# Moving a sign merge of the weight rounding from VectorE to GpSimd in every other piece

## The chip, the cores and the metric

The kernel runs on one core of a Trainium2 chip. The metric is the device time of one execution in microseconds (us): the median of three runs of the kernel before is 1490.21 us (1490.04 to 1492.53). The profile shown below is of one execution whose span is 1490.6 us.

The core's engines each work through a list of instructions in a fixed order: TensorE (PE) multiplies matrices, VectorE (DVE) does elementwise work and sorting steps, ScalarE (ACT) does activations and copies, GpSimd (POOL) does elementwise work more slowly, SyncE (SP) issues the transfers (DMA). [...]

## What is computed

```python
scores = scale * np.matmul(q, k.transpose(0, 1, 3, 2))      # 8 x 8 heads, 576 x 576 each
kth = np.partition(scores, -32, axis=-1)[..., -32:-31]
scores = np.where(scores >= kth, scores, -1e9)              # the 32 largest of each row stay
attn = softmax(scores)                                       # in words: exp, divided by the row's sum
x = (attn @ v), laid out as 4608 tokens x 512
h = x @ w_in                                                 # 512 x 2048
out = np.maximum(0.01 * h, h) @ w_out                        # 2048 x 512
```

The weights `w_in` and `w_out` arrive as float64. The kernel takes each as four 16-bit words and makes the float32 itself: that is the weight rounding, and the change is in it.

## The kernel before

**The opening.** The two weight matrices are cut into 16 pieces (`NPIECE`) of 128 x 1024 numbers, 1 MB each as float64. `load_weights` (L95 to L102) brings a piece into a tile `raw`, of which there are three buffers. `round_weights` (L104 to L149) is a Python generator that emits one piece's rounding in three steps:

- Step 0. GpSimd copies the highest of the four words of each number into a dense tile `top` (L119). ScalarE turns the second word into a part of the significand (L120, straight into the weight tile) and the two lowest words into another (L122).
- Step 1. VectorE takes the exponent out of `top` (L124), clamps it (L126); ScalarE shifts it to the place of a bfloat16's exponent (L128; for the last two pieces VectorE does it, L130). The result, `scale`, is a power of two written as a bfloat16. VectorE makes the leading bits of the significand (L131) and then leaves in `top` only the sign bit (L132). TensorE adds the three parts of the significand up in PSUM (L142 to L144).
- Step 2. VectorE puts the sign into `scale` with a bitwise or of two 16-bit tiles (L146), and multiplies the sum in PSUM by it (L149). The product is the float32 weight.

The loop at the end of the kernel runs the steps as a software pipeline: in round n it emits step 0 of piece n, step 1 of piece n-1, step 2 of piece n-2, and then the load of piece n+3. Each engine executes its own part of this in the order written. So VectorE's list repeats a block of six: L124, L126, L131, L132 of one piece, then L146 and L149 of the piece before it.

`top` and `scale` have two buffers each. A tile of piece n takes the place of piece n-2's, so GpSimd's copy L119 of piece n waits until L146 of piece n-2 has read its `top`. Rounds 6 to 9 also load queries and keys; round 13 and the end of the loop compute the scores of the first two attention units (`first_scores`), whose copies (L231) go through ScalarE's list.

**The main part.** After the rounding, 144 attention units follow, one a slot. VectorE finds the 32 largest of each row (L240, L245, L248), GpSimd masks (L258, L259), ScalarE takes exponents, normalizes and splits the result into 16-bit halves (tile `split`, two buffers, L283) for a transposing transfer; TensorE computes scores, weighs the values (L323), and runs the matrix products with the weights (L374, L386) in between. VectorE begins this part only when its list of the rounding is empty.

Of the kernel before, what the change touches and what calls it, by code (L numbers as in the profile page):

```python
# [10 lines left out]
U16 = mybir.dt.uint16  # L11
BF16 = mybir.dt.bfloat16
AF = mybir.ActivationFunctionType
ALU = mybir.AluOpType
# [5 lines left out]
def kernel(  # L20
# [13 lines left out]
    nc = tc.nc  # L34
    NPAIR, P, S = qT.shape
# [14 lines left out]
    WCH = 1024  # L50
# [10 lines left out]
    raws = ctx.enter_context(tc.tile_pool(name="raws", bufs=3))  # L61
    work = ctx.enter_context(tc.tile_pool(name="work", bufs=2))
# [20 lines left out]
    AS_WORDS = weights.dtype != F32  # L83

    def piece(n):

        if n < NPIECE // 2:
            j, c = divmod(n, HP)
            return w_in[c][:, j * WCH:(j + 1) * WCH]
        f = 2 * (n - NPIECE // 2)  # L90
        return w_out[f // 4][:, f % 4:f % 4 + 2, :].rearrange("p g n -> p (g n)")
# [3 lines left out]
    def load_weights(n):  # L95
        if n >= NPIECE:
            return
        if not AS_WORDS:
            nc.sync.dma_start(piece(n), weights[n])
            return  # L100
        raw_of[n] = raws.tile([P, WCH, 4], U16, name="raw")
        nc.sync.dma_start(raw_of[n].rearrange("p n w -> p (n w)"), weights[n])  # L102

    def round_weights(n):  # L104

        raw = raw_of.pop(n)  # L110
        dst = piece(n)
        mid = raw[:, :, 2]
        low = raw.rearrange("p n w -> p (n w)").bitcast(U32).rearrange("p (n w) -> p n w", w=2)[:, :, 0]
        top = raws.tile([P, WCH], U16, name="top", bufs=2)
        scale = raws.tile([P, WCH], U16, name="scale", bufs=2)
        parts = work.tile([P, 2 * NKC - 1, P], F32, name="wT", bufs=3)
        parts = parts.rearrange("p c n -> p (c n)").bitcast(U16)
        m_top, m_low = parts[:, 0:WCH], parts[:, WCH:2 * WCH].bitcast(BF16)
        nc.gpsimd.tensor_copy(top, raw[:, :, 3])  # L119
        nc.scalar.activation(dst, mid, AF.Copy, bias=-7.0 - 2.0 ** -16, scale=2.0 ** -20)  # L120

        nc.scalar.activation(m_low, low, AF.Copy, bias=128.0, scale=2.0 ** -29)  # L122
        yield
        nc.vector.tensor_scalar(scale, top, 4, 0x7FF, ALU.logical_shift_right, ALU.bitwise_and)  # L124

        nc.vector.tensor_scalar(scale, scale, 1151.0, 896.0, ALU.min, ALU.max)  # L126
        if n < NPIECE - 2:
            nc.scalar.activation(scale, scale, AF.Copy, bias=-896.0 * 128, scale=128.0)  # L128
        else:
            nc.vector.tensor_scalar(scale, scale, 896.0, 128.0, ALU.subtract, ALU.mult)  # L130
        nc.vector.tensor_scalar(m_top, top, 0xF, 0x3F80, ALU.bitwise_and, ALU.bitwise_or)  # L131
        nc.vector.tensor_scalar(top, top, 0x8000, None, ALU.bitwise_and)  # L132
        if n < NPIECE - 4 or n % 2 == 0:
            tag, bufs = ("wide", 2) if n < NPIECE - 4 else ("narrow", 1)
            pw = ps_sc.tile([P, 2, 512], F32, name=tag, bufs=bufs)
            sums = [(pw[:, h, :], h * 512) for h in range(2)]
            ends = [(pw.rearrange("p h n -> p (h n)"), 0)]
        else:
            ends = sums = [(ps_ml.tile([P, 512], F32, name="pw", tag="ml"), h * 512) for h in range(2)]
        for pw, c in sums:  # L140
            at = slice(c, c + 512)
            nc.tensor.matmul(pw, ident_top, m_top[:, at].bitcast(BF16), start=True, stop=False)  # L142
            nc.tensor.matmul(pw, ident, dst[:, at], start=False, stop=False)
            nc.tensor.matmul(pw, ident_low, m_low[:, at], start=False, stop=True)  # L144
        yield
        nc.vector.tensor_tensor(scale, scale, top, ALU.bitwise_or)  # L146
        for pw, c in ends:
            at = slice(c, c + pw.shape[-1])
            nc.vector.tensor_tensor(dst[:, at], pw, scale[:, at].bitcast(BF16), ALU.mult)  # L149
# [5 lines left out]
    def load_qk(pi):  # L155
        qt = loads.tile([P, S], F32, name="qt")
        kt = loads.tile([P, S], F32, name="kt")
        nc.sync.dma_start(qt, qT[pi])
        nc.sync.dma_start(kt, kT[pi])
        qk_of[pi] = qt, kt  # L160
# [58 lines left out]
    def first_scores(u):  # L219

        ps = [ps_sc.tile([P, 2, 512], F32, name="wide", bufs=2) for i in range(2)]
        for half in range(2):
            for i, pi, side, r0 in u.parts:
                qt, kt = qk_of[pi]
                d = slice(side * D, (side + 1) * D)
                nc.tensor.matmul(ps[i][:, half, 0:HS], qt[d, u.q0:u.q0 + P],
                                 kt[d, half * HS:(half + 1) * HS], start=True, stop=True)
        u.both = work.tile([P, 2, S], F32, name="s_sb", bufs=5)
        u.s = [u.both[:, i, :] for i in range(2)]
        for i in range(2):  # L230
            nc.scalar.copy(u.s[i].rearrange("p (h n) -> p h n", h=2), ps[i][:, :, 0:HS])  # L231
# [201 lines left out]
    def unit(n):  # L433
        return steps[n] if 0 <= n < len(steps) else None
# [26 lines left out]
    with tc.manual_schedule():  # L461
        last = {p: n for n, u in enumerate(steps) for p in u.pairs}

        def load_more(s):

            for of, load, n, lag in ((qk_of, load_qk, LOADED, -2), (v_of, load_v, LOADED_V, LAG + 1)):
                while len(of) < NPAIR and (len(of) < n or last[len(of) - n] + lag <= s):
                    load(len(of))


        for n in range(3):
            load_weights(n)
        rounding = {}
        for n in range(NPIECE + 2):
            for i in (n, n - 1, n - 2) if AS_WORDS else ():
                if 0 <= i < NPIECE:
                    if i == n:
                        rounding[i] = round_weights(i)
                    next(rounding[i], None)
            load_weights(n + 3)  # L480
            if 6 <= n < 6 + HP:
                load_qk(n - 6)
            elif n == NPIECE - 3:
                first_scores(steps[0])
            elif n == NPIECE:
                first_scores(steps[1])
            if n == NPIECE - 1:
                load_v(0)
                load_v(1)

        def values(s):
            due = [u for n, u in enumerate(steps) if values_at(n) == s]
            if due:
                po = ps_sc.tile([P, 2, 512], F32, name="wide", bufs=2)[:, 0, 0:2 * P]
                po = po.rearrange("p (u n) -> p u n", u=2)
            else:
                return
            for part in (weigh_values, keep_values):
                for n, u in enumerate(due):
                    part(u, po[:, n, :])  # L500
            attended(s)

        for s in range(len(steps) + LAG + 1):
            cur, old, older, new = unit(s), unit(s - 1), unit(s - 2), ()
            if s % 2 == 0:
                new = [u for u in steps[s + 2:s + 4] if u]
            picks = top_k(cur) if cur else iter(())
            budget = slot_budget(s)

            def slot():  # L510
                next(picks, None)

            slot()
            if old:
                mask(old, 0)
                mask(old, 1)
            if older:
                reciprocals(older)
                normalize(older, 0)
                normalize(older, 1)  # L520
            mlp_steps(budget)
            slot()
            if s - 2 in HURRIED:
                transpose_in_haste(older)
            mlp_steps(budget)
            if old:
                exponents(old, 0)
            if older:
                keep_transposed(older) if s - 2 in HURRIED else transpose(older)
            slot()  # L530
            mlp_steps(budget)
            mlp_steps(budget)
            slot()
            mlp_steps(budget)
            if old:
                exponents(old, 1)
                sums(old)
            if new and s < HURRY:
                scores(new)
            values(s)  # L540
            if new and s >= HURRY:
                scores(new)
            budget = slot_budget(s + 1)
            mlp_steps(budget)
            mlp_steps(budget)
            load_more(s)
        mlp_steps(1e9)
# [58 lines left out]
```

## Time and profile before

| Stretch of the span, us | PE busy | DVE busy | ACT busy | POOL busy | DMA share |
|---|---|---|---|---|---|
| 0 to 13.3 (first pieces) | 5.29 | 4.29 | 8.67 | 4.19 | 0.86 |
| 13.3 to 69.5 (rounding, steady) | 43.47 | 52.10 | 42.05 | 14.82 | 0.79 |
| 69.5 to 113 (first attention units) | 7.92 | 43.15 | 22.95 | 30.14 | 0.22 |
| 113 to 1440 | 1298.33 | 1229.35 | 1017.21 | 1048.48 | 0.54 |
| 1440 to 1490.6 | 46.83 | 0.00 | 4.75 | 0.00 | 0.03 |

Each cell but the last column is the time in us in which the engine had an instruction in flight during the stretch; the last column is the mean busy share of the core's 16 DMA engines. The stretches were chosen where the work changes: at 13.3 us VectorE writes its first finished weights, at 69.5 us it begins with the attention. An engine whose busy time fills a stretch is a candidate for what sets its length; whether it does is told by the chain of waits, not by this table.

### The profile page before, as it was taken

The numbers are of one execution on the slowest core, as the hardware profiler recorded it, in microseconds if no ns is written. First come the engines' busy times: TensorE is split into PE (matmuls) and PEld (weight loads), VectorE is DVE, ScalarE is ACT, GpSimd is POOL, SyncE is SP. The second block draws the span as 40 slices with busy tenths as digits, with TensorE's granted clock in tenths as the row PEclk, the third lists the DMA queues.
The fourth block names the chain that finished last, engine by engine and source line by source line (L and its number), as shares of the span: only waits on it lengthen the run. The fifth ranks groups of instructions, "written<-read, shape, count | busy, mean of one in ns | idle before, by whom it ended". The sixth has DMA issues, their size and how long they took to land.

```text
span 1490.6 us, 24127 instructions
## 1 busy us (share of the span) xinstructions
PE 1401.8 (94%) x8077; PEld 934.0 (63%) x8077; DVE 1328.9 (89%) x3414; ACT 1095.6 (74%) x1979; POOL 1097.6 (74%) x742
## 2 busy tenths in 40 slices
PE   6708977999999999999999999999999999999998
PEld 2305546666666766676766666767676767676674
DVE  7999998999999999999999999999999999999600
ACT  8647786777788877777777777777777777777720
POOL 2277787888788887788887888888878887788700
PEclk9968997999999999999999999999999999999999
DMA  8623354635566566655564566545765465645510
GB/s 325 249 64 84 99 166 122 169 110 145 156 162 160 142 163 170 171 134 165 168 177 126 137 168 171 164 142 155 177 163 142 130 168 147 169 128 142 143 47 14
DMA packets 386172, 221.12 MB, mean 148 GB/s; under 512 B 331520, under 2 KB 331520, under 8 KB 384000
## 3 DMA queue, kind: packets, MB, share of 16 engines
q1 hardware_dynamic: 386048, 219.59, 52.5%
q8 instruction: 63, 1.03, 0.3%
q14 instruction: 61, 0.50, 0.1%
HBM read 46.14 MB, written 91.42 MB: 92 GB/s over the span
## 4 chain that ended last, share of the span: by engine, by line
PE 84%; DVE 6%; ACT 4%; DMA 4%; issue 1%; SPq 0%; POOL 0%; DVEq 0%; ACTq 0%
PE pz L386 34%; PE ph L374 28%; PE wide L323 11%; PE wide L210 6%; PE narrow L210 3%; DMA wT<-apart 2%; ACT split L283 2%; DMA apart<-split 1%; DVE tops L245 1%; ACT s_sb L274 1%; DVE pairs L248 1%; ACT s_sb L262 1%; PE ph L348 1%; DVE w_out L149 1%; DVE w_in L149 1%
## 5 line engine op out<-in xcount | busy, mean ns | idle before, releaser
L258 POOL TENSOR_SCALAR pen<-s_sb,tops 128x576 f32<-128x576 f32 x288 | 638.3, 2216 | 223.7 <-DVE tops L245 136.0
L245 DVE MAX8 tops<-pairs 128x8 f32<-128x288 f32 (+1 forms) x1152 | 636.4, 592 | 0.0
L386 PE MATMUL pz<-w_out,gT 128*128 128x512 f32 x1152 | 508.3, 596 | 1.4 <-ACT gT L359 1.4
L374 PE MATMUL ph<-x,w_in 128*128 128x256 f32 x2176 | 481.1, 381 | 0.0
L248 DVE MATCH_REPLACE8 pairs<-tops,pairs 128x288 f32<-128x288 f32 (+1 forms) x864 | 460.5, 539 | 0.0
L374 PEld LDWEIGHTS ph<-x,w_in 128*128 128x128 f32 x2176 | 410.7, 190 | 77.1 <-issue 22.9
L259 POOL TENSOR_TENSOR s_sb<-s_sb,pen 128x576 f32<-128x576 f32 x288 | 406.8, 1413 | 24.0
L386 PEld LDWEIGHTS pz<-w_out,gT 128*128 128x128 f32 x1152 | 215.3, 190 | 266.2 <-issue 263.4
L283 ACT COPY split<-s_sb 128x1152 uint16<-128x1152 uint16 x278 | 304.8, 1145 | 0.0
L262 ACT ACTIVATE s_sb<-s_sb,nbias 128x576 f32<-128x576 f32 x288 | 221.1, 768 | 12.4 <-POOL s_sb L259 12.4
L274 ACT ACTIVATE s_sb<-s_sb,rz 128x576 f32<-128x576 f32 x288 | 207.1, 770 | 25.6 <-DVE rz L271 25.6
L240 DVE TENSOR_TENSOR pairs<-s_sb 128x576 f32<-128x576 f32 x288 | 213.7, 780 | 9.9
L323 PEld LDWEIGHTS wide<-wT,vt 128*64 128x64 f32 x3200 | 164.5, 141 | 66.0 <-issue 18.7
L323 PE MATMUL wide<-wT,vt 128*64 128x128 f32 (+1 forms) x3200 | 183.3, 271 | 23.2 <-ACT s_sb L217 15.1
L337 ACT COPY x<-wide 128x128 f32<-128x128 f32 (+1 forms) x160 | 32.3, 261 | 153.3 <-PE wide L323 153.3
L210 PE MATMUL wide<-kt,qt 64*128 64x352 f32 (+1 forms) x632 | 118.3, 488 | 27.5 <-ACT s_sb L217 22.0
L380 ACT ACTIVATE gT<-ph 128x512 f32<-128x512 f32 x136 | 80.7, 593 | 78.8 <-PE ph L374 78.8
L217 ACT COPY s_sb<-wide 128x704 f32<-128x704 f32 x142 | 107.0, 754 | 21.7 <-PE wide L210 21.7
L210 PEld LDWEIGHTS wide<-kt,qt 64*128 64x128 f32 (+1 forms) x632 | 48.6, 178 | 44.8 <-ACT s_sb L217 22.5
L210 PE MATMUL narrow<-kt,qt 64*128 64x224 f32 (+1 forms) x632 | 69.1, 358 | 7.7 <-DMA kt<-in_kT_dram 7.7
L271 DVE RECIPROCAL rz<-ze 128x2 f32<-128x2 f32 x144 | 22.5, 156 | 60.2 <-ACT ze L267 60.0
L217 ACT COPY s_sb<-narrow 128x448 f32<-128x448 f32 x142 | 68.7, 536 | 5.6 <-PE narrow L210 4.9
(58 smaller groups left out, 551.0 us busy)
## 6 DMA issues: line engine op xcount, KB each, us to landing
apart<-split SPq DMA_DIRECT2D x278, 288.0 KB, 2.1
raw<-in_weights_dram SPq DMA_DIRECT2D x16, 1024.0 KB, 6.0
vt<-in_vk_dram SPq DMA_DIRECT2D x32, 320.0 KB, 3.3
qt<-in_qT_dram SPq DMA_DIRECT2D x32, 288.0 KB, 3.7
kt<-in_kT_dram SPq DMA_DIRECT2D x32, 288.0 KB, 4.0
out_dram<-o_sb SPq DMA_DIRECT2D x36, 256.0 KB, 2.0
wT<-apart SPq DMA_TRANSPOSE x139, 4.6
```

The lines of the kernel that those rows point to most:

```text
L210: nc.tensor.matmul(to[r0:r0 + u.rows, i, :], qt[d, u.q0:u.q0 + u.rows], kt[d, k0:k1], start=True, stop=True)
L240: nc.vector.tensor_tensor(pairs[:, :, n, :], u.both[:, :, 0:HS], u.both[:, :, HS:S], op)
L245: nc.vector.max(out=u.tops[:, i, r, :], in_=rest[i])
L248: nc.vector.match_replace(out=rest[i], in_to_replace=u.tops[:, i, r, :], in_values=rest[i], imm_value=LOWEST)
L258: nc.gpsimd.tensor_scalar(pen, u.s[i], u.tops[:, i, ROUNDS - 1, 7:8], MASKED, ALU.is_lt, ALU.mult)
L259: nc.gpsimd.tensor_tensor(u.s[i], u.s[i], pen, ALU.add)
L262: nc.scalar.activation(u.s[i], u.s[i], AF.Exp, bias=u.nbias[:, i:i + 1], scale=SCALE, accum_out=u.z[:, i:i + 1])
L274: nc.scalar.activation(u.s[i], u.s[i], AF.Copy, bias=0.0, scale=u.rz[:, i:i + 1])
L283: nc.scalar.copy(split, pairs[:, :, h])
L323: nc.tensor.matmul(po[side * D:(side + 1) * D, o, :], vt[:, c, side, :], u.wT[:, c + side * NKC if c + 1 < NKC else c, r:r + n], start=(c ...
L374: nc.tensor.matmul(ph[:, i, 0:n], w_in[c][:, f * P:(f + 1) * P], x[c][:, 0:n], start=(c == 0), stop=(c == HP - 1),)
L386: nc.tensor.matmul(pz[0:m, 0:DMODEL], gT[:, f, r0:r0 + m], w_out[f // 4][:, f % 4, :], start=(f == 0), stop=(f == NFC - 1),)
```

## The change

The sign merge of step 2 moves to GpSimd for the odd pieces. There, VectorE's L132 leaves not the bare sign bit but the bfloat16 number +1 or -1 (sign bit, and the bits 0x3F80 of 1.0), and GpSimd multiplies `scale` by it as bfloat16 numbers, which puts the sign on the power of two. Even pieces keep the bitwise or on VectorE. The aim is to take an instruction off VectorE's block in every other piece.

So that GpSimd's list can run further ahead, the highest words get four buffers in all: two of the tile `top` as before, and, for pieces with n % 4 of 2 or 3, the two buffers of the attention's tile `split`, which is not in use yet. The copy L119 of piece n then waits for the reader of piece n-4's words. The generator gets a fourth step: the product of piece n-2 is emitted first in round n, ahead of the copy of piece n in GpSimd's list; VectorE's L146 and L149 stay at the round's end.

```diff
-        top = raws.tile([P, WCH], U16, name="top", bufs=2)
+        if n % 4 < 2:
+            top = raws.tile([P, WCH], U16, name="top", bufs=2)
+        else:
+            top = work.tile([P, 2 * S], U16, name="split", bufs=2)[:, 0:WCH]
...
-        nc.vector.tensor_scalar(top, top, 0x8000, None, ALU.bitwise_and)
+        if n % 2:
+            nc.vector.tensor_scalar(top, top, 0x8000, 0x3F80, ALU.bitwise_and, ALU.bitwise_or)
+        else:
+            nc.vector.tensor_scalar(top, top, 0x8000, None, ALU.bitwise_and)
...
         yield
-        nc.vector.tensor_tensor(scale, scale, top, ALU.bitwise_or)
+        if n % 2:
+            nc.gpsimd.tensor_tensor(scale.bitcast(BF16), scale.bitcast(BF16), top.bitcast(BF16), ALU.mult)
+        yield
+        if n % 2 == 0:
+            nc.vector.tensor_tensor(scale, scale, top, ALU.bitwise_or)
...
-            for i in (n, n - 1, n - 2) if AS_WORDS else ():
+            for i in (n - 2, n, n - 1, n - 2) if AS_WORDS else ():
```

## The prediction

> **What bounds the kernel now.** I read the table of stretches first (in the section on the profile), then the chain of waits of the first 130 us, then VectorE's and GpSimd's lists in order of time. The diff touches only the opening, and there the chain, followed back from 130 us, runs through VectorE from 13.3 to 69.5 us without a break. One block of it, from the chain (start, time on the chain, what):
>
> ```profile
> 22.09 0.44 DVE scale L124
> 22.55 0.43 DVE scale L126
> 22.98 0.35 DVE wT L131
> 23.35 0.43 DVE top L132
> 23.77 0.61 DVE scale L146
> ...
> 24.48 1.24 DVE w_in L149
> 25.81 0.44 DVE scale L124
> ```
>
> L124 to L132 belong to piece 4, L146 and L149 to piece 3. The block repeats after 25.81 - 22.09 = 3.72 us, as it does until 59 us, and VectorE waits for nothing in it. Start to start in VectorE's list (L132 at 23.35, L146 at 23.69), the four 16-bit instructions take 1.60 us ("the four" from here on), L146 0.79, L149 1.33. The rest has room: ScalarE's three take about 3.05 (L128 starts at 10.14, 13.11 and 16.15), TensorE's six 2.58.
>
> GpSimd is idle two thirds of the time, but look at when it runs (start, duration, then what ended its idle time):
>
> ```profile
> 5.60 1.10 POOL L119 COPY top<-raw 128x1024 uint16<-128x1024 uint16 x1 [4.31 <-DMA raw<-in_weights_dram]
> 8.09 1.30 POOL L119 COPY top<-raw 128x1024 uint16<-128x1024 uint16 x1 [1.39 <-DMA raw<-in_weights_dram]
> ...
> 20.72 1.14 POOL L119 COPY top<-raw 128x1024 uint16<-128x1024 uint16 x1 [2.58 <-DVE scale L146]
> 24.44 1.15 POOL L119 COPY top<-raw 128x1024 uint16<-128x1024 uint16 x1 [2.57 <-DVE scale L146]
> ```
>
> In the steady state each copy starts as L146 ends and lies wholly beside L149 (24.48 to 25.71). The wait for `top`, 2.6 us a time, keeps the copies out of the way of the four. The only copy that met one of them is the second: it started at 8.09 inside L132 (7.99 to 8.42) and took 1.30, not 1.10.
>
> After 69.5 us everything starts from VectorE's first L240, so I count each us gained or lost in the opening as one us of the end.
>
> [...]
>
> Does the trace show the exclusion? GpSimd waiting for VectorE: yes, the 1.30 us copy. VectorE waiting for GpSimd: the main part shows it for the two-input L240 (two of them in the row of 948.88, which take about 1.5 elsewhere):
>
> ```profile
> 948.88 1.80 DVE L240 TENSOR_TENSOR pairs<-s_sb 128x576 f32<-128x576 f32 x2
> ```
>
> ```profile
> 948.67 2.22 POOL L258 TENSOR_SCALAR pen<-s_sb,tops 128x576 f32<-128x576 f32 x1 [2.19 <-ACT split L283]
> ```
>
> L240 by itself takes 745 ns; the longest of all 288 takes 1136 and is the first of these two, with L258 begun 0.21 us before it. It was held 0.39 us, to 0.60 after L258's start, not for L258's whole 2.22. So the exclusion is real[...]. That one of the four[...] is held to GpSimd's end is not shown anywhere here.
>
> [...] L259, two f32 inputs of 576, takes 1.41[...].
>
> **The change, part by part.**
>
> - *L146 gone for odd pieces*: -0.79 us a block in every other block. A pair of blocks would take 2 x 3.72 - 0.79 = 6.65 instead of 7.44.
> - *L132 with a second operation*: L124 has two operations and 0.43 us, L132 one and 0.43. Nothing.
> - *The product on GpSimd*: not in the trace. Nearest row: L259, 1.41 x 1024/576 = 2.51. Low end 1.14, a copy of as many 16-bit elements with one input; high end 3.94, L258 by elements (2216 ns x 1024/576). I take 2.5: same instruction[...].
> - *Four buffers*: L119 loses its wait for L146. Copies, and with them the release of `raw`, come earlier, but nothing on the chain waits for either; what they do is move the copies out from beside L149.
> - *New waits*: the product waits for L128 and L132 of its piece; behind it in GpSimd's list stand the copies of the next two pieces, on which L124 of those pieces hangs. L149 of an odd piece waits for the product; behind it is VectorE's whole list.
>
> GpSimd's work per pair is 2.5 + 2 x 1.12 and three gaps of 0.1, 5.0 us, beside a pair of 6.65. If nothing contended it would fit. With exclusion I walk one pair, time 0 at L124 of an odd piece. The four end at 1.60. L146 of the even piece before runs 1.60 to 2.28[...]. L128 of the odd piece is done at 0.92 + 1.06 = 1.98, so the product starts as L146 ends, 2.32, beside L149 (starts 2.39), and ends at 4.83. VectorE wants its next four at 3.72: it **waits 1.11**. They run 4.83 to 6.43, then L149 of the odd piece to 7.76. The first queued copy [...] runs to about 7.6; the second follows at 7.7, just ahead of the next L124, and ends at 8.85: VectorE **waits 1.1** again. The pair takes 8.9 us: 7.44 - 0.79 + 1.11 + 1.1. Should L124 win that race instead, the second copy falls behind the next L146 and the product behind the copy, and the wait that the product causes grows by about the same 1.1: again 8.9.
>
> So +1.45 us a pair. Of the eight products, the first (piece 1) falls where VectorE waits for a cold TensorE anyway (1.42 us at 13.32), so I count seven: 7 x 1.45 = +10.2. At the very end L149 of piece 15 can start 0.43 + 2.5 + 0.1 = 3.03 after L132's start at 65.26; before it started at 68.31, 3.05 after. That end is a wash. Likeliest: 1490.2 + 10.2 = **1500.4**.
>
> **The rivals.**
>
> - *No hold on the four by GpSimd* (faster). For: the hold on L240 ended after 0.6 of 2.2 us, and no trace here shows one of the four held. Against: [...]the copy held by L132. Then six products save 0.79, -4.7; piece 13's comes late, because its L128 stands behind the first scores' copies in ScalarE's list (it ran at 60.23 before, 3.8 us after the end of its L126), and 2.6 us of product replace 0.79 of L146: +0.9, half of the difference, as all of ScalarE's list also moves ahead. Sum -3.8: 1486.4; from 1484.7 (seven savings) to 1489.
> - *Half a hold*: [...] The two waits shrink to 0.7 and 0.9: pair 8.25, +0.8 x 7 = +5.7: 1495.9.
> - *A worse order*: both copies fall between the four, not beside L149. Pair 6.65 + 1.11 + 2 x 1.12 = 10.0, +2.56 x 7 = +18: 1508. For it: the four have gaps of some hundredths between dependent ones, in which a queued copy could get in. Against: a copy that is ready as the four end falls beside L149 by itself.
>
> A product of 1.14 or 3.94 us would shift the likeliest case by about -1.1 x 7 = -8 (the first wait gone) or +1.4 x 7 = +10[...].
>
> **How the numbers follow.** Full hold 0.41, half a hold 0.22, worse order 0.10, no hold 0.27. "Faster" (under 1487.2) takes 0.16 of the no-hold case, "same" its other 0.11 and 0.05 of a half hold with a quick product; the rest, 0.68, is slower. The range 1486 to 1508 leaves out the better part of no hold, about 0.1, and the slower part of the worse order with a slow product, about 0.1.
>
> **What would show it.** The start of VectorE's first L240, 69.52 before, should be about 80, and the end should move with it. In the steady opening the block should alternate, with idle time before L124 or L126[...]: GpSimd's product or a copy in flight up to the moment at which it starts, or durations well above 0.43. If the four keep 0.43 us beside a running product and the pair takes 6.65, the no-hold case is right and I am wrong. If the product takes far from 2.5 us, the sum is off by that. A shift of L240 that the end doesn't show would refute the one-for-one count.

## The result, and the profile after

The changed kernel takes 1505.38 us (median; 1503.49 to 1505.64), against 1491.37 us for the kernel before on the same chip: 1.0089 times as long, interval 1.0072 to 1.0107. That is 13.3 us more (10.7 to 16.0). Its profiled span is 1503.4 us, 12.8 more than before.

In the lines of the changed kernel, the four are L127, L129, L134 and L136 or L138 (L136 in odd pieces, with the second operation); the even pieces' merge is L156, the multiplication out of PSUM L159, ScalarE's shift of the exponent L131, GpSimd's copy L122, its product L153, the first attention instruction L250.

The table of stretches, cut at 13.3 us as before and at VectorE's first attention instruction, tells where the time is (the stretch and its length, PE busy, PE loads, DVE, ACT, POOL, each with its number of instructions, then the TensorE clock, DMA share, GB/s). The first line is of the kernel before, the second of the changed one:

```profile
13.30:69.50 56.20, 43.47 (x136) 17.64 (x135) 52.10 (x91) 42.05 (x42) 14.82 (x13) 1.00 0.79 303
13.30:82.70 69.40, 49.35 (x133) 19.75 (x133) 60.21 (x84) 41.73 (x42) 33.63 (x21) 0.88 0.66 247
```

The stretch lasts 69.4 us instead of 56.2. So a loss of 13.2 us is made in the rounding, and the span's 12.8 says that it is carried to the end. VectorE has fewer instructions there (84 for 91), yet its busy time has *grown*, from 52.1 to 60.2 us. So 8.1 us of the loss show up as busy time and don't look like a wait; the other 5.1 are idle time, 4.13 of it in one wait at the end of the rounding. The clock column, 1.00 before and 0.88 now, is a second thing to come back to.

The chain of waits of the same block that the prediction opened with (start, time on the chain, what):

```profile
24.49 0.86 DVE scale L127
25.38 1.20 DVE scale L129
26.57 1.25 DVE wT L134
28.19 1.23 DVE w_in L159
29.51 0.44 DVE scale L127
```

Three of the four, 0.43 us each before, show 0.86, 1.20 and 1.25, and the block takes 29.51 - 24.49 = 5.02 us instead of 3.72. Why, is told by VectorE's and GpSimd's instructions in order of time (start, duration; in brackets idle time and what ended it):

```profile
22.37 0.69 DVE L156 TENSOR_TENSOR scale<-scale,split 128x1024 uint16<-128x1024 uint16 x1
...
22.89 2.17 POOL L153 TENSOR_TENSOR scale<-scale,split 128x1024 bf16<-128x1024 bf16 x1 [3.64 <-DMA raw<-in_weights_dram]
23.16 1.23 DVE L159 TENSOR_TENSOR w_in<-wide,scale 128x1024 f32<-128x1024 f32 x1
...
24.49 0.85 DVE L127 TENSOR_SCALAR scale<-top 128x1024 uint16<-128x1024 uint16 x1
...
25.00 1.28 POOL L122 COPY top<-raw 128x1024 uint16<-128x1024 uint16 x1
25.38 1.20 DVE L129 TENSOR_SCALAR scale<-scale 128x1024 uint16<-128x1024 uint16 x1
26.23 1.29 POOL L122 COPY split<-raw 128x1024 uint16<-128x1024 uint16 x1
...
26.49 1.32 DVE L134 TENSOR_SCALAR wT<-top 128x1024 uint16<-128x1024 uint16 x1
...
27.85 0.43 DVE L138 TENSOR_SCALAR top<-top 128x1024 uint16<-128x1024 uint16 x1
```

Follow GpSimd. Its product of piece 3 starts at 22.89, 0.08 us after its exponent L131 is done (21.75 + 1.06) and while piece 2's merge L156 is still in flight (the bracket names a transfer, which the product doesn't read; in the next pairs it names L131). It lies beside L159 without harm (1.23, as ever), and ends at 25.06. L127 begins inside it and ends at 25.34; it takes 0.42 longer than its 0.43. The copy of piece 5 follows and ends at 26.28; L129 takes 1.20. The copy of piece 6 ends at 27.52; L134 takes 1.32. Then GpSimd's list is empty and L138 has its 0.43. Each of the three gets through as one GpSimd instruction ends and, while it runs, holds the next one up: the copies take 1.28 and 1.29, against 1.10 to 1.16 in the kernel before, away from the four. The three rows name neither idle time nor a releaser: a held instruction has started, has no idle time before it, and is counted as busy.

### The profile page after: what moved, and what is told of

The parts are those of the page before. It is cut to its first block, busy times and chain, and to the rows that moved or that the text cites. A ratio compares the mean times of both kernels' runs of the same rounds, so it can differ in the third digit from the quotient of the medians.

```text
span 1503.4 us, 24132 instructions
## 1 busy us (share of the span) xinstructions
PE 1408.3 (94%) x8077; PEld 934.9 (62%) x8077; DVE 1338.2 (89%) x3406; ACT 1095.4 (73%) x1979; POOL 1115.0 (74%) x750
## 3 DMA queue, kind: packets, MB, share of 16 engines
q1 hardware_dynamic: 386048, 219.59, 52.1%
## 4 chain that ended last, share of the span: by engine, by line
PE 84%; DVE 5%; ACT 5%; DMA 5%; issue 1%; POOL 0%; SPq 0%; DVEq 0%; ACTq 0%
PE pz L396 33%; PE ph L384 27%; PE wide L333 11%; PE wide L220 6%; PE narrow L220 3%; DMA wT<-apart 3%; ACT split L293 2%; DMA apart<-split 1%; ACT s_sb L284 1%; DVE tops L255 1%; ACT s_sb L272 1%; DVE pairs L258 1%; PE ph L358 1%; DVE scale L129 1%; DVE wT L134 1%
## 5 line engine op out<-in xcount | busy, mean ns | idle before, releaser
L250 DVE TENSOR_TENSOR pairs<-s_sb 128x576 f32<-128x576 f32 x288 | 213.5, 780 | 9.9
L333 PE MATMUL wide<-wT,vt 128*64 128x128 f32 (+1 forms) x3200 | 181.3, 270 | 22.1 <-ACT s_sb L227 14.5
```

Source lines behind the costliest of these rows:

```text
L250: nc.vector.tensor_tensor(pairs[:, :, n, :], u.both[:, :, 0:HS], u.both[:, :, HS:S], op)
L333: nc.tensor.matmul(po[side * D:(side + 1) * D, o, :], vt[:, c, side, :], u.wT[:, c + side * NKC if c + 1 < NKC else c, r:r + n], start=(c ...
```

## The experiments

VectorE's first attention instruction is the yardstick for the opening (69.52 before). For all runs:

| Kernel | First attention instruction, shift in us | Run against the kernel before, us (interval) |
|---|---|---|
| the change | +13.2 | +13.3 (10.7 to 16.0) |
| e1, four buffers alone | +3.7 | +6.0 (4.0 to 7.9) |
| e2, product, two buffers | +15.5 | +14.5 (12.1 to 16.8) |
| e3, odd signs left out | -1.8 | -1.5 (-2.8 to -0.1) |
| e4, product in every piece | +20.0 | +21.8 (19.5 to 23.8) |
| e5, product up to piece 11 | +12.0 | +15.0 (13.1 to 17.1) |
| e6, even copies on ScalarE | +13.1 | +12.5 (9.4 to 15.5) |
| e7, idle product added | +9.1 | +9.5 (7.7 to 11.3) |
| e8, first scores later | +9.1 | +10.9 (8.2 to 13.6) |
| e9, spare matmuls | +12.0 | +13.3 (10.6 to 15.9) |
| e10, odd signs left out, gate kept | -4.0 | -5.4 (-7.3 to -3.3) |
| v1, merge in one instruction | +1.5 | +2.8 (1.5 to 4.0) |

The run's column is the ratio less one, times the median of the kernel before, measured beside it (1488.96 to 1491.37). The first column comes from one profiled run of each kernel. Both columns go together over a range of some 25 us, within about 3 us in each row: what the opening loses, the end loses.

**Does GpSimd hold the four up, or do they wait for data?** A product that nobody reads, on one of the attention's tiles, was added to the kernel before; merge and copies stay as they were.

```diff
         nc.vector.tensor_scalar(top, top, 0x8000, None, ALU.bitwise_and)
...
+        if n % 2 and n < NPIECE - 2:
+            idle = work.tile([P, 2 * S], U16, name="split", bufs=2)[:, 0:WCH]
+            nc.gpsimd.tensor_tensor(idle.bitcast(BF16), parts[:, 0:WCH].bitcast(BF16), parts[:, 0:WCH].bitcast(BF16), ALU.mult)
```

> The kernel before, with a bf16 product of 128x1024 on GpSimd added for the odd pieces 1 to 13, whose result nobody reads and on which nothing waits but GpSimd's next copy; the sign merge stays on VectorE. In GpSimd's list it stands behind a copy that starts with the multiplication on VectorE, so it starts about 0.2 us before the next piece's four and lasts 2.2. Theory of the hold: the first of the four is held to about 0.13 us before its end, 1.8 to 1.9 us a pair, so about +12 to +13 us in seven pairs. Rival, the loss came from the waits for the product's result: 0, at most +1.

In its trace in order of time (L142 is the product, L119 a copy, L152 the multiplication):

```profile
38.65 1.13 POOL L119 COPY top<-raw 128x1024 uint16<-128x1024 uint16 x1 [2.59 <-DVE scale L149]
...
39.73 1.90 POOL L142 TENSOR_TENSOR split<-wT 128x1024 bf16<-128x1024 bf16 x1
...
40.02 1.90 DVE L124 TENSOR_SCALAR scale<-top 128x1024 uint16<-128x1024 uint16 x1
```

L124 depends on nothing that the product makes, and takes 1.90 instead of 0.43: it began inside the product and ended 0.29 after it. The pair of blocks takes 8.91 us (36.30 to 45.21, starts of L124), 7.44 + 1.47, from piece 4 on, and the run 9.5 us more. That is less than the 12 to 13 expected: the product took 1.90 us and not 2.2, and seven pairs at 1.47 come to 10.3. The hold is shown, with no wait for data in it; its cause isn't. How long it lasts, the traces tell: in the changed kernel's block above, the three held 16-bit `tensor_scalar` end 0.28, 0.30 and 0.29 us after the GpSimd instruction they began in, and 0.43 is what they need alone, so they are held to within some 0.15 us of its end. The L240 of the prediction was held to 0.60 of 2.22 us.

**Is the product needed for the loss, and are the buffers?** The four buffers alone, on the kernel before:

```diff
-        top = raws.tile([P, WCH], U16, name="top", bufs=2)
+        if n % 4 < 2:
+            top = raws.tile([P, WCH], U16, name="top", bufs=2)
+        else:
+            top = work.tile([P, 2 * S], U16, name="split", bufs=2)[:, 0:WCH]
```

> Four buffers for the highest words, the sign merge left on VectorE for all pieces and the order of the steps as before. The copies on GpSimd then no longer wait for the merge and lose their place beside the multiplication of the PSUM sum. Theory of the hold (a GpSimd instruction in flight holds VectorE's 16-bit tensor_scalar instructions until about its own end): a copy of 1.1 us costs nothing where it falls beside the multiplication and up to 0.9 us where it falls among the four; with a third to a half of 14 copies falling badly, the first attention instruction of VectorE (69.5 us before) comes 3 to 6 us later and the run takes +3 to +6 us. Rival, the buffers alone are the cause of the loss: +10 us or more. Rival, only the new waits for the product cost anything: 0.

It is 6.0 us slower (4.0 to 7.9), with no product and no instruction more. The copies no longer wait for L146 but for the transfers, start when these land, and so fall among the four here and there: the longest of the first, second and third of the four take 1.16, 1.22 and 1.32 us. And the other way round, the changed kernel with the two old buffers of `top`:

```diff
-        if n % 4 < 2:
-            top = raws.tile([P, WCH], U16, name="top", bufs=2)
-        else:
-            top = work.tile([P, 2 * S], U16, name="split", bufs=2)[:, 0:WCH]
+        top = raws.tile([P, WCH], U16, name="top", bufs=2)
```

> The change with two buffers for the highest words in place of four. The copy for an even piece then waits for the merge of the even piece before it and lies beside the multiplication, but the product behind it in GpSimd's list starts later. Theory of the hold: the product now holds the first of the next four as in the run with the idle product (about 1.5 us), the copy behind it the second (about 0.8): 2.3 us a pair in place of 2.1, a pair of about 8.9 us, and a run of +13 to +16 us, like the change. Rival, the four buffers brought a good part of the loss: +8 us or less.

14.5 us slower (12.1 to 16.8), which the interval doesn't tell from the change; its pairs take 8.7 to 9.4, 9.2 on average, where 8.9 was expected. With the product there, the number of buffers hardly matters; without it, the buffers do harm.

**What was the wait worth that kept the copies beside L149?** The kernel before without the merge for odd pieces, whose weights so lose their signs:

```diff
-        nc.vector.tensor_tensor(scale, scale, top, ALU.bitwise_or)
+        if n % 2 == 0:
+            nc.vector.tensor_tensor(scale, scale, top, ALU.bitwise_or)
```

> The kernel before with the sign merge of the odd pieces left out altogether (their weights lose their signs), nothing put on GpSimd, two buffers. This is what the change hoped to gain, without its price. All theories: a pair of pieces takes 7.44 - 0.79 = 6.65 us, the first attention instruction comes 5 to 6.3 us earlier than 69.5, and if the opening counts one for one in the end the run takes about 1485.5 us. Rival, the main part is bound by something that swallows the opening's gain: under 2 us gained in the end.

Eight instructions of 0.69 us are gone, and the opening gains 1.8 us, a third of what was expected. The trace in order of time (L147 is the merge left in even pieces):

```profile
26.60 0.68 DVE L147 TENSOR_TENSOR scale<-scale,top 128x1024 uint16<-128x1024 uint16 x1
26.75 1.51 POOL L119 COPY top<-raw 128x1024 uint16<-128x1024 uint16 x1 [4.53 <-DVE top L132]
...
28.64 1.10 POOL L119 COPY top<-raw 128x1024 uint16<-128x1024 uint16 x1 [0.39 <-DVE w_in L150]
...
28.72 1.32 DVE L124 TENSOR_SCALAR scale<-top 128x1024 uint16<-128x1024 uint16 x1
```

Look at what releases the copies. The one at 26.75 was released by L132, ahead of the merge, and the next one follows in the same block, at 28.64, just ahead of L124, which takes 1.32. Before, each merge released one copy, and so each block had one, beside its multiplication; with every other merge gone they come in twos, and the second falls among the four. The merge had done a second thing: by its place it released a copy at the right moment. So it was left out again, with an instruction that costs next to nothing in its place (odd signs are missing here too):

```diff
         if n % 2 == 0:
             nc.vector.tensor_tensor(scale, scale, top, ALU.bitwise_or)
+        else:
+            nc.vector.tensor_scalar(top[:, 0:8], top[:, 0:8], 0x8000, None, ALU.bitwise_and)
```

> The kernel before with the sign merge of the odd pieces left out (their weights lose their signs), but with an instruction of 128x8 on the same tile in its place, so that the copy that takes that tile's place still waits until then and lies beside the multiplication. Theory that the gain of the run without the merge (1.8 us in the opening, of 6.3 that were saved on VectorE) was lost to copies that now began earlier and held the four: no hold remains, a pair takes about 6.8 us, first attention instruction at 64 to 65 us in place of 67.7 and 69.5, run -4 to -6 us. Rival, the transfers or ScalarE limit a faster opening: 67 to 68 us, run -1 to -2 us, as without the gate.

Its trace in order of time:

```profile
28.91 0.16 DVE L149 TENSOR_SCALAR top<-top 128x8 uint16<-128x8 uint16 x1
28.98 1.22 DVE L152 TENSOR_TENSOR w_in<-wide,scale 128x1024 f32<-128x1024 f32 x1
...
29.14 1.12 POOL L119 COPY top<-raw 128x1024 uint16<-128x1024 uint16 x1 [2.05 <-DVE top L149]
...
30.31 0.43 DVE L124 TENSOR_SCALAR scale<-top 128x1024 uint16<-128x1024 uint16 x1
```

The small L149 takes 0.16 us, the copy starts behind it and lies beside the multiplication L152, and the four keep their 0.43 throughout. The pair takes 6.72 us, and the run is 5.4 us faster (3.3 to 7.3), against 1.5 in e3. From piece 10 on a pair takes 8.0: the copies then wait for the transfers (2.60 to 2.89 us), so with these buffers a still quicker VectorE would gain little here. It is no usable kernel, but it measures the prize the change was after.

**More products, and copies elsewhere.** The product in all pieces, no merge at all on VectorE:

```diff
-        if n % 2:
-            nc.vector.tensor_scalar(top, top, 0x8000, 0x3F80, ALU.bitwise_and, ALU.bitwise_or)
-        else:
-            nc.vector.tensor_scalar(top, top, 0x8000, None, ALU.bitwise_and)
+        nc.vector.tensor_scalar(top, top, 0x8000, 0x3F80, ALU.bitwise_and, ALU.bitwise_or)
...
-        if n % 2:
+        if True:
             nc.gpsimd.tensor_tensor(scale.bitcast(BF16), scale.bitcast(BF16), top.bitcast(BF16), ALU.mult)
         yield
-        if n % 2 == 0:
-            nc.vector.tensor_tensor(scale, scale, top, ALU.bitwise_or)
```

> The change with the product on GpSimd in every piece, and no merge on VectorE at all. Theory of the hold: VectorE's block is 2.93 us without the merge; the product (2.16 us, started 1.98 after the block) holds the first of the next four by about 1.0 and the copy behind it the second by about 0.8, so a piece takes about 4.75 us in place of 3.72 before and 4.37 with the change; first attention instruction 16 to 20 us late, run about +18 us. Rival, the saving on VectorE outweighs from some dose on: less than the change's +13.

Its trace in order of time (L150 is the product):

```profile
29.13 2.13 POOL L150 TENSOR_TENSOR scale<-scale,top 128x1024 bf16<-128x1024 bf16 x1 [1.52 <-ACT scale L131]
...
29.94 1.61 DVE L127 TENSOR_SCALAR scale<-top 128x1024 uint16<-128x1024 uint16 x1
...
31.21 1.28 POOL L122 COPY split<-raw 128x1024 uint16<-128x1024 uint16 x1
31.59 1.20 DVE L129 TENSOR_SCALAR scale<-scale 128x1024 uint16<-128x1024 uint16 x1
```

The block takes 4.88 us where 4.75 were expected: each product holds L127 (1.61, so 1.18 more), each copy L129 (1.20, 0.77 more). The run is 21.8 us slower (19.5 to 23.8).

If every second copy leaves GpSimd's list, a pair should lose one hold. The changed kernel with the even pieces' copies on ScalarE:

```diff
-        nc.gpsimd.tensor_copy(top, raw[:, :, 3])
+        if n % 2 == 0 and n > 0:
+            nc.scalar.copy(top, raw[:, :, 3])
+        else:
+            nc.gpsimd.tensor_copy(top, raw[:, :, 3])
```

> The change with the copies of the highest words of pieces 2, 4, ... 14 made on ScalarE in place of GpSimd. One GpSimd instruction fewer to hold the four in each pair. Theory of the hold: the hold of 0.9 us on the third of the four goes, the holds by the product (0.4) and by the other copy (0.8) stay; ScalarE has 7.1 us of work a pair; a pair takes about 7.8 us in place of 8.74, and TensorE's gaps shrink below 3 us, so that most of the extra at the end goes too: first attention instruction 5 to 8 us late, run +5 to +8 us. Rival, the waits for the product's result carry the loss: unchanged, +13.

It missed: pairs of 8.4 to 9.2 us between pieces 4 and 12, a run as slow as the change. L134's hold did go, but ScalarE, with a copy more, delivers the exponent later, the product starts later, and holds more of the first of the four (L130 here; its trace in order of time):

```profile
40.51 2.13 POOL L156 TENSOR_TENSOR scale<-scale,split 128x1024 bf16<-128x1024 bf16 x1 [5.54 <-ACT scale L134]
...
41.02 1.91 DVE L130 TENSOR_SCALAR scale<-top 128x1024 uint16<-128x1024 uint16 x1
```

A product that starts 0.51 before L130, not 1.60 before L127 as in the change, holds it 1.48 us, the longest of these holds; the others take 0.8 to 1.2, against 0.42 in the change. What one hold lost, another gained in the main.

**The end of the rounding.** In the changed kernel VectorE stands still there. In order of time:

```profile
67.16 1.24 PE L236 MATMUL wide<-kt,qt 64*128 64x288 f32 x8
...
68.44 1.18 ACT L241 COPY s_sb<-wide 128x576 f32<-128x576 f32 x2 [5.84 <-PE wide L236]
...
71.59 1.04 ACT L131 ACTIVATE scale<-scale 128x1024 uint16<-128x1024 uint16 x1
...
72.71 2.13 POOL L153 TENSOR_TENSOR scale<-scale,top 128x1024 bf16<-128x1024 bf16 x1 [10.25 <-ACT scale L131]
...
74.88 1.29 DVE L159 TENSOR_TENSOR w_out<-pw,scale 128x512 f32<-128x512 f32 x2 [4.13 <-POOL scale L153]
```

Piece 13's product waits for its exponent, L131, which ScalarE reaches only at 71.59, behind the copies L241 of the first scores; those wait for matmuls L236 at 67.16. VectorE's L159 waits 4.13 us for the product. In the kernel before, L128 came at 60.23, in time for the merge at 61.35. Three runs took this apart. First, no product in the last pieces:

```diff
-        if n % 2:
+        if n % 2 and n < 12:
             nc.vector.tensor_scalar(top, top, 0x8000, 0x3F80, ALU.bitwise_and, ALU.bitwise_or)
...
-        if n % 2:
+        if n % 2 and n < 12:
             nc.gpsimd.tensor_tensor(scale.bitcast(BF16), scale.bitcast(BF16), top.bitcast(BF16), ALU.mult)
         yield
-        if n % 2 == 0:
+        if n % 2 == 0 or n >= 12:
```

> The change with the product on GpSimd for pieces 1 to 11 alone; pieces 13 and 15 keep the merge on VectorE. In the changed kernel the first attention instruction came 13.2 us late, of which 3.9 us were lost after the start of piece 14's four. Theory that these 3.9 are a cost of its own (VectorE waits 4.1 us for piece 13's product, whose exponent stands behind the first scores' copies on ScalarE): about +9 us in place of +13. Rival, they come from the matmuls of pieces 12 to 15 running late and slow, and would be there without the late products: still +12 to +13.

It missed: +9 was expected. The opening ends 1.2 us sooner and the run doesn't show it (15.0 us slower, 13.1 to 17.1). Now piece 13's merge on VectorE waits 1.60 us for the same L131: the late exponent is the trouble, not only the product behind it. Second, the first scores' work one round later, behind that exponent in ScalarE's list:

```diff
-            elif n == NPIECE - 3:
+            elif n == NPIECE - 2:
                 first_scores(steps[0])
```

> The change with the scores of the first attention unit issued one round later, so that ScalarE's shift of piece 13's exponent no longer stands behind their copies. In the changed kernel VectorE waited 4.1 us for piece 13's product, and 3.9 us were lost after piece 14's four. Theory that this order in ScalarE's list is the cause: the wait falls to 1 us or less, first attention instruction 79 to 80 us in place of 82.7, run +10 in place of +13. Rival, the late and slow matmuls behind the held instructions are: 82 us or later, run unchanged.

VectorE's last instruction of the rounding and its first of the attention, in order of time:

```profile
77.39 1.29 DVE L159 TENSOR_TENSOR w_out<-pw,scale 128x512 f32<-128x512 f32 x2 [0.66 <-POOL scale L153]
...
78.59 0.75 DVE L250 TENSOR_TENSOR pairs<-s_sb 128x576 f32<-128x576 f32 x1
```

The wait of 4.13 us is gone; what remains is 0.66 for piece 15's product. From piece 14's first instruction (68.39) to the first attention instruction it takes 10.20 us, against 10.23 before and 14.09 in the change. The order in ScalarE's list is what cost the 4 us. (The edit was not tried on the kernel before.) Third, why the matmuls of the first scores came late. TensorE's list in order of time in the changed kernel:

```profile
36.60 0.61 PE L148 MATMUL wide<-wT,ident_top 128*128 128x512 bf16 x1 [3.05 <-DVE wT L134]
...
37.00 1.92 PE L149 MATMUL wide<-w_in,ident 128*128 128x512 f32 x2
```

After 3.05 us without work, the matmul L148 takes 0.61 us instead of 0.38, and the two of L149 1.92 instead of 1.02 (both from the blocks without a gap): that is the clock of 0.88. VectorE's held L134 feeds these matmuls, so the holds starve TensorE, and slow matmuls follow. Of its six gaps of 1.9 to 3.1 us between 18 and 63 us, four were followed by such slow matmuls. The granted clock was 0.50 from 36.6 to 39.6 us and 1.00 from 40 to 43; from start to start a slow bf16 matmul of 128x512 takes 0.43 us (20.02 to 20.45), a quick one 0.22 (23.68 to 23.90). The length of the gap alone doesn't tell: gaps of 2.08, 2.78 and 3.05 us (twice) were followed by the slow clock, and those of 1.89 and 2.52 weren't. What sets it off isn't shown. Spare matmuls that fill the gaps tell what it cost:

```diff
             nc.tensor.matmul(pw, ident_low, m_low[:, at], start=False, stop=True)
+        if n < NPIECE - 4:
+            spare = ps_ml.tile([P, 512], F32, name="spare", tag="ml")
+            for i in range(8):
+                nc.tensor.matmul(spare, ident_top, m_top[:, 0:512].bitcast(BF16), start=True, stop=True)
```

> The change with eight spare bf16 matmuls of 128x512 (1.7 us by the rows of the trace) behind the matmuls of each of pieces 0 to 11, into a PSUM tile that nobody reads. In the changed kernel TensorE idles up to 3.05 us while the instruction that it waits for is held, and the matmuls after such a gap run at half speed. Theory that the gaps are what slows them: with gaps of 1.3 us all matmuls from piece 2 on take 0.22 and 0.43 us start to start, VectorE's waits for TensorE in the opening (0.38, 0.18, 0.54 us) go, piece 12's six matmuls take 2.6 in place of 4.4 us; first attention instruction 79.5 to 81.5 us in place of 82.7. Rival, the slow matmuls are not on the path that sets the opening's length: 82.5 us.

TensorE's list in order of time at one of the former gaps:

```profile
60.99 1.89 PE L154 MATMUL spare<-wT,ident_top 128*128 128x512 bf16 x8
...
62.86 0.38 PE L148 MATMUL narrow<-wT,ident_top 128*128 128x512 bf16 x1
```

The eight spare ones (L154) fill the gap, and the next L148 takes 0.38. Every pair of blocks now takes 8.77 or 8.78 us (8.5 to 9.1 in the change), and the wait for piece 13's product falls from 4.13 to 2.88. The opening ends 1.2 us sooner; the run time (13.3 us slower, 10.6 to 15.9) can't tell so little. The slow clock was a by-product worth about 1.2 us of the opening, the holds and ScalarE's order the rest.

**A version without GpSimd.** If VectorE's list is the limit and GpSimd can't help, the merge could absorb L132: one instruction that masks `top` and puts the sign on.

```diff
-        nc.vector.tensor_scalar(top, top, 0x8000, None, ALU.bitwise_and)
...
-        nc.vector.tensor_tensor(scale, scale, top, ALU.bitwise_or)
+        nc.vector.scalar_tensor_tensor(scale, top, 0x8000, scale, ALU.bitwise_and, ALU.bitwise_or)
```

> A version that may beat both: nothing on GpSimd but the copies, two buffers, and on VectorE one scalar_tensor_tensor, (top and 0x8000) or scale, in place of the two instructions that leave the sign in top (0.34 us start to start) and merge it (0.79). The copy waits for its end and so keeps its place beside the multiplication. If it runs at the rate of the merge (0.69 us): a block of 3.38 us, first attention instruction about 5 us early, run about -5 us. [...]: a block of about 3.9 us, +2 to +3 us.

Groups of instructions of its opening (L145 is the new one; count, then busy time and mean ns of one, then idle time before):

```profile
L145 DVE SCALAR_TENSOR_TENSOR scale<-top,scale 128x1024 uint16<-128x1024 uint16 x16 | 19.5, 1219 | 0.9 <-ACT scale L128 0.9
```

1219 ns where the two that it replaces take 427 and 684: 2.8 us slower (1.5 to 4.0). No version that was run and computes all of the weights beats the kernel before.

## Why the prediction was right, and where its sum was not

1500.4 us was forecast, 1505.4 came, inside the range and slower, as forecast. The mechanism, GpSimd holding up the four, was right; that the steady pair fitted so well is luck, as two of its steps were wrong and cancel. By steps:

- *What bounds the opening.* Right: VectorE's list. e10 took some 0.7 us off every other block and gained 5.4 us.
- *The saving of 0.79 a pair.* Right, by e10: 6.72 us a pair without holds, where 6.65 was worked out.
- *The hold on the four by GpSimd.* Right, and shown by e7. That it lasts to GpSimd's end was the author's estimate: the kernel before showed 0.60 us on L240 and the copy of 1.30. The case of no hold is out. Half a hold isn't told apart from a whole one: L240's 0.60 us for 576 elements, scaled to 2048 and 1024, gives an estimate of 2.1 us for a product and 1.0 for a copy, nearly all of what they last here. What is out is a hold as short as L240's 0.60 us.
- *The product at 2.5 us, from L259.* It measured 2.13 to 2.17 in the steady opening, some 0.35 us less. L259's 1.41 us for 576 elements of 32 bits gives an estimate of 2.51 for 1024 if scaled by elements, 1.25 if scaled by bytes; 1024 of 16 bits took 2.15, nearer to the first.
- *The order in a pair.* Wrong. The product was to be followed by the four, the first copy beside L149, the second in front of the next four. In fact both copies ran among the four, the order of the rival called worse: the walk had no GpSimd instruction start before the four had ended (an estimate), but a waiting copy gets in behind the first of them (one started at 25.00, L129 at 25.38). There it was costed as if each copy held VectorE for all of its 1.12; in fact the instructions between run while the next GpSimd instruction is held, so each copy cost 0.77 and 0.90. And the product's hold was 0.42, not 1.11: it is shorter by 0.35, starts 0.17 us before L156 ends instead of after it, and the held L127 needs only 0.28 us past its end. The sum hardly moved, by luck: holds of 0.42 + 0.77 + 0.90 = 2.09 against 2.21, pair 33.23 - 24.49 = 8.74 us against 8.9.
- *Four buffers at nothing on the chain.* Right that nothing waits for the copies; wrong to call it free. e1 makes them worth +6.0 us by themselves (+3.7 in the opening of its profiled run), because they take the copies away from beside the multiplication.
- *The first product at nothing.* The largest miss. It was to fall where VectorE waits for TensorE's slow first matmuls (the two of L143 took 1.91 us at 10.95 in the kernel before, 1.02 at 14.92). That wait (0.34 us now) ends at 13.01, before the multiplication L159; the product starts at 14.38, after it, and holds L129 for 1.80 us, and its two copies hold 0.90 and 0.80. From piece 2's first instruction to piece 4's it takes 24.49 - 14.34 = 10.15 us, against 7.44: +2.71. The prediction's own figures said so: its L128 of 13.11 is piece 1's, on which this product waits, and with 1.04 us it ends at 14.15. In the changed kernel, in order of time:

```profile
14.38 2.37 POOL L153 TENSOR_TENSOR scale<-scale,top 128x1024 bf16<-128x1024 bf16 x1 [2.59 <-ACT scale L131]
...
14.79 2.23 DVE L129 TENSOR_SCALAR scale<-scale 128x1024 uint16<-128x1024 uint16 x1
```

- *The last two products at 1.45 each.* They cost 14.09 - 10.23 = 3.86, not 2.9. For piece 15 the prediction's "wash" held for the product itself: its L159 starts 3.04 us after its L136, as L149 did 3.05 after L132; but the sum counts it at 1.45. Piece 13's cost 4.13 - 0.79 = 3.34 alone. The prediction had seen its late exponent, but used it in the case of no hold only.
- *One for one to the end.* Right: 13.2 us at the first attention instruction, 12.8 in the span, 13.3 in the run.

The sum by stretches, from the starts of the first of the four: up to piece 2 -0.31; piece 2 to 4 +2.71; piece 4 to 12, four pairs, 35.02 - 29.76 = +5.26 (4 x 1.45 = 5.8 forecast); piece 12 to 14, 9.09 - 7.44 = +1.65 (1.45); from there to the first attention instruction +3.86 (2.9). Together +13.17. The five us that the forecast fell short are 2.4 at the first product and 1.0 at the last two, less 0.3 in the pairs between; the rest, some 2 us, lies between the two medians of the kernel before (1490.2 and 1491.4) and within the interval.

What stays open: what causes the hold isn't shown, and whether the four would escape it in another form, at a longer duration of their own, wasn't tried. Nor do the runs show why one gap of 2.5 us on TensorE left its clock alone and one of 2.1 didn't.

## What to carry to other kernels

GpSimd, busy for 14.82 of 56.20 us in the rounding of the kernel before, wasn't free capacity here: its instructions held up those of the engine that bounds, by 0.42 to 0.90 us each in the block shown. Cost new work by what it holds up, and look for the hold as longer durations, not as idle time. Before taking away an instruction or a wait, look up what it releases and when; here a wait of 2.6 us that cost nothing kept the copies where they did no harm, and an instruction of 0.16 us in the same place was worth 2 us of the opening and 4 of the run. The first and the last round of a pipeline deserve their own walk: most of the forecast's error lay there.

## What the runs showed of the hardware, not expected

- In the changed kernel the held 16-bit `tensor_scalar` ended 0.27 to 0.30 us after the GpSimd instruction that held them, less than their own 0.43. Thirteen copies on GpSimd that began while one of the four was in flight took 1.28 to 1.33 us, where 1.10 to 1.16 is usual in the kernel before; one, begun in the last 0.08 us of L134 (10.68), took 1.10.
- The product on GpSimd took 1.90 us with one tile as both inputs (e7) and 2.13 to 2.17 with two, where VectorE's bitwise or of two such tiles (L156) took 0.69; the first and the last of the changed kernel, which started 0.04 and 0.23 us after one of VectorE's 16-bit instructions had, took 2.37 and 2.43.
- TensorE ran at half speed (granted clock 0.50, a bf16 matmul of 128x512 every 0.43 us and not every 0.22) after four of six gaps: those of 2.08, 2.78 and twice 3.05 us, not those of 1.89 and 2.52.
- `scalar_tensor_tensor` took 1219 ns for 1024 16-bit elements, as long as the multiplication of as many f32 out of PSUM (1225), where `tensor_tensor` took 684 and `tensor_scalar` 427.
